# A fused attention and MLP block in fp32 on one core: the first T tile moves to second place in a unit's first step, and ScalarE copies the outputs of the last unit but one

## The chip, the cores and the metric

The kernel runs on one core of a Trainium2 chip. The engines that matter here are TensorE (PE in the profile, its weight loads PEld), VectorE (DVE), ScalarE (ACT), GpSimd (POOL) and SyncE (SP), which issues most DMAs. The metric is the device time of one execution in microseconds, the median of several runs. The kernel before took 1554.22 us (three runs, 1554.19 to 1554.6).

## The reference

```python
xn = layernorm(x)                                # 2048 tokens x 512
q, k, v = split(xn @ wqkv)                       # 32 heads of 16
o = softmax(q @ k.T * 16**-0.5) @ v              # per head, 2048 x 2048 scores
s = o @ wo
g = silu(gelu(xn @ w1 + b1) @ w2 + b2)           # 512 -> 1376 -> 512
return x + s * g
```

All of it is fp32. The scores are large, so the softmax subtracts each row's maximum, and the kernel therefore makes every score twice: once to take the maximum, once, transposed, for the exponential.

## The kernel before, in words

The program is written in a fixed order by hand; no scheduler moves anything. It has two stretches.

The first, up to about 470 us, does the layer norm, the projections and the MLP, and on the side a part of the first scores with their maxima. The second is a loop over n = 0 to 512, one step each. The heads are in 8 groups of four, the queries in 4 chunks of 512; a group and a chunk make a unit u (32 units), and a unit has 16 steps, one for each block of 128 keys. n = 16u is the first step of unit u.

A step is a string of letters (`ORDER`, and `FIRST` in the first step of a unit), each letter one piece of work for TensorE and what follows from it:

- **T** (four in a step, `t_one`, L713): 128 keys x 512 queries of transposed scores of one head, with the negated maximum as two more rows of the contraction. They go to the PSUM banks `ps` (the first T, here T0), `two` (T1 and T2 together) and `pst` (T3). ScalarE takes the exponential of each bank into a buffer `slot` (L716, L718). T0 and T2 use the lower 64 rows of TensorE's array (`SIDES`, second number 1), T1 and T3 the upper 64.
- **S** (L192): a whole 128 x 512 tile of scores of a later unit, whose row maxima VectorE takes (L198). In a step of three such tiles the first S (S0) is on the upper rows, the second (S1) on the lower.
- **X** and **Y** (L192): two half tiles of 256 columns, X on the upper rows, Y on the lower, in one bank; the reduction comes after Y. Ahead of Y a TensorE nop waits for X to be done (`hold`).
- **V** (`pv_step`, L784): probabilities times values of the step before, four matmuls side by side in the bank `pv`, summed over the 16 steps of a unit.

S, X and Y share three banks in a ring, so each of them waits until VectorE has reduced what stood in its bank. The sums in `pv` are complete with the V of step 16u, which belongs to unit u - 1; they are copied to `os` (L791), and the V of step 16u + 1 may only start when that copy is done, since there is one bank `pv`. The first T0 and the first T1 of a unit also wait for the DMAs that loaded its queries and maxima (`qt`), four DMA queues each; these waits are instructions of TensorE's own queue (EVENT_SEMAPHORE).

How many score tiles a step has is set by `due`: three in nearly every step up to n = 490, none after that. `FIRST` is used where a unit's first step has three, that is in units 5 to 30, 26 times. In the first steps of units 1 to 4 there are two, and the order is `ORDER[2]`, which begins with T.

From n = 492 on, without score tiles, the steps hold products with the output weights for the first ten token blocks instead (`w_halves`, L911), with ScalarE's rounding copies (L889) and tanh (L845), VectorE's gates (L846, L917) and GpSimd's differences and sums (L892, L922). The last copy of `pv` but one, that of unit 30, falls in step 496.

```python
ORDER = {0: "TTTTV", 2: "TSTTSTV", 3: "XTSTTYSTV"}
SIDES = ((1, 1), (0, 0), (0, 1), (1, 0))
        order = ORDER[want] if n > 1 else ("TTTTV", "TSTTSVT")[n]
        if want == 3 and ka == 0:
            order = FIRST
```

Of the kernel before, what the change touches and what calls it, by code (L numbers as in the profile page):

```python
# [10 lines left out]
AF = mybir.ActivationFunctionType  # L11
# [27 lines left out]
HB = 4  # L39
W2B = 2  # L40
ORDER = {0: "TTTTV", 2: "TSTTSTV", 3: "XTSTTYSTV"}
FIRST = "SXTTTSYTV"
SOON = 580
FEW = 4
SIDES = ((1, 1), (0, 0), (0, 1), (1, 0))
# [8 lines left out]
def fused(ctx: ExitStack, tc: tile.TileContext, x, wqk, wv, wo, w1, b1, w2, b2, out):  # L54
    nc = tc.nc
# [43 lines left out]
    NU = NG * NCH  # L99
# [677 lines left out]
    PV, OS, DN, DR = {}, {}, {}, {}  # L777
    def pv_step(u, k):
        g = u // NCH
        if k == 0:  # L780
            PV[u] = ps_v.tile([P, CH], F32, name="pv")
        for j in range(GH):
            h = (g * GH + j) * VW
            nc.tensor.matmul(PV[u][32 * j:32 * j + 32, :], vsb[:, k, h:h + 32], PT[u, k][:, j, :],  # L784
                             start=(k == 0), stop=(k == NT - 1))
        del PT[u, k]
        if k == NT - 1:
            OS[u] = wb.tile([P, CH], F32, name="os", bufs=1)
            pv = PV.pop(u)
            if u < NU - 1:  # L790
                nc.vector.tensor_copy(OS[u], pv)  # L791
            else:
                nc.scalar.activation(OS[u][:, :HC], pv[:, :HC], AF.Copy)
                nc.vector.tensor_copy(OS[u][:, HC:], pv[:, HC:])
# [189 lines left out]
    for n in range(L + 1):  # L984
        ua, ka = divmod(n, 16)
        want = due(n) - due(n - 1)
        i = 0
        if put_off and ka > 1:
            s_turn(*put_off.pop(0))
        else:  # L990
            for u in list(ended):
                if u >= PAIRED or ka > 2 and since.setdefault(u, n) < n:
                    s_end0(u)
# [3 lines that stand above are left out]
        for op in order:  # L997
            if op in "SXY":
                s_op(op)
            elif op == "V":  # L1000
                if n:
                    pv_step(*divmod(n - 1, 16))
                for _ in range(4):
                    tick()
                flush()
            else:
                if EARLY <= 4 * n + i < 4 * L:
                    t_one(ua, ka, i, True)
                for f, args in todo.get((n, i), []):
                    f(*args)  # L1010
                i += 1
# [54 lines left out]
```

## Time and profile before

| | |
|---|---|
| median of the runs | 1554.22 us |
| the profiled execution | 1554.05 us |
| its span, first to last instruction | 1552.3 us |
| granted TensorE clock, mean | 1.000 |
| busy: PE, DVE, ACT, POOL | 1544.9, 1415.1, 1214.2, 367.7 us |

The profiled execution lies within 0.2 us of the median, and 1.75 us of its time lie outside the span. Busy times of PE are no sign of a full TensorE, since matmuls overlap and their ends are modelled. A row of the timeline gives the start in us, the busy time of the row, engine, line, operation, output and input tile, shape and count; in square brackets stands the idle time of the engine ahead of the row and what ended it. Rows of the same kind that overlap are put together (x2). A row of the waits gives who waited for whom, us in total, times, longest.

### The profile page before, as it was taken

What the parts mean: (1) busy time and instruction counts of PE and PEld (TensorE: products, weight loads), DVE (VectorE), ACT (ScalarE), POOL (GpSimd) and SP (SyncE); (2) the same over time, 40 slices, a digit from 0 to 9 for tenths busy, and PEclk for the clock granted to TensorE, in tenths of its full rate; (3) what the DMA queues carried; (4) which work ended last, traced back from release to release, by engine and by line L of the source; (5) the groups of instructions that cost most, each with busy time, mean ns of one, the idle gap of its engine ahead of it and who ended that gap; (6) DMA issues with size and microseconds to landing.
All of it is one profiled execution on the core that took longest, in us unless ns stands there. A gap on an engine that the chain in (4) does not pass through costs nothing.

```text
span 1552.3 us, 31308 instructions
## 1 busy us (share of the span) xinstructions
PE 1544.9 (100%) x12242; PEld 926.8 (60%) x12242; DVE 1415.1 (91%) x2295; ACT 1214.2 (78%) x1881; POOL 367.7 (24%) x370
## 2 busy tenths in 40 slices
PE   9999999999999999999999999999999999999999
PEld 8899999999994444444444444444444444444455
DVE  7599999999998999999999999999999999999834
ACT  4333433434339999999999999999999999999984
POOL 4145675765741001001000100100010000000143
PEclk9999999999999999999999999999999999999999
DMA  6625443454422113113311411411041111110153
GB/s 211 154 60 146 129 140 100 145 152 122 130 85 77 44 36 67 30 37 61 66 28 30 70 37 36 69 34 29 23 81 29 33 30 32 41 30 22 48 197 115
DMA packets 78643, 116.83 MB, mean 75 GB/s; under 512 B 28036, under 2 KB 28292, under 8 KB 77320
## 3 DMA queue, kind: packets, MB, share of 16 engines
q1 hardware_dynamic: 74748, 101.89, 23.8%
q0 software_dynamic: 3264, 12.35, 4.7%
q8 instruction: 96, 1.57, 0.4%
q10 hardware_dynamic: 484, 0.60, 0.1%
q14 instruction: 51, 0.42, 0.1%
HBM read 84.35 MB, written 25.97 MB: 71 GB/s over the span
## 4 chain that ended last, share of the span: by engine, by line
PE 98%; DVE 1%; DMA 0%; ACT 0%; issue 0%; DVEq 0%
PE pv L784 33%; PE ps L192 22%; PE ps L582 13%; PE two L713 8%; PE sp L582 5%; PE pst L713 4%; PE ps L713 4%; PE pst L582 3%; PE pv L582 2%; PE ps L911 2%; PE ps L91 1%; PE ps L454 1%; PE pst L91 0%; DVE st L413 0%; PE two L91 0%; DMA xt<-in_x 0%
## 5 line engine op out<-in xcount | busy, mean ns | idle before, releaser
L198 DVE TENSOR_REDUCE mx<-ps 128x2 f32<-128x512 f32 x2048 | 1318.5, 687 | 75.3 <-PE ps L192 25.8
L784 PE MATMUL pv<-slot,vsb 128*32 128x512 f32 x4096 | 545.4, 605 | 0.9 <-DVE os L791 0.9
L718 ACT ACTIVATE slot<-two 128x1024 f32<-128x1024 f32 x511 | 520.4, 1018 | 4.3 <-PE pst L713 3.7
L192 PEld LDWEIGHTS ps<-kt,slot 48*128 48x128 f32 x1364 | 214.2, 185 | 295.8 <-DVE mx L198 285.0
L192 PE MATMUL ps<-kt,slot 48*128 48x256 f32 (+1 forms) x1364 | 374.8, 364 | 0.0
L716 ACT ACTIVATE slot<-ps 128x512 f32<-128x512 f32 x515 | 307.1, 597 | 18.0 <-PE ps L713 6.6
L716 ACT ACTIVATE slot<-pst 128x512 f32<-128x512 f32 x511 | 309.5, 606 | 0.6 <-PE ps L713 0.6
L582 PE MATMUL ps<-slot,w1h 64*128 64x512 f32 x1088 | 222.9, 393 | 0.0
L713 PE MATMUL two<-qt,kt 50*128 50x512 f32 x766 | 202.4, 399 | 0.3 <-DVE gt L642 0.3
L192 PE MATMUL ps<-kt,qz 48*128 48x512 f32 x512 | 202.5, 396 | 0.0
L713 PE MATMUL ps<-qt,kt 50*128 50x512 f32 x387 | 190.4, 494 | 0.0
L192 PEld LDWEIGHTS ps<-slot,slot 48*128 48x128 f32 x594 | 93.7, 184 | 126.3 <-DVE mx L198 121.5
L192 PE MATMUL ps<-slot,slot 48*128 48x256 f32 (+1 forms) x594 | 164.8, 364 | 0.0
L582 PEld LDWEIGHTS ps<-slot,w1h 64*128 64x128 f32 x1088 | 155.0, 186 | 8.8
L784 PEld LDWEIGHTS pv<-slot,vsb 128*32 128x32 f32 x4096 | 80.9, 108 | 131.0 <-issue 121.4
L582 PE MATMUL ps<-slot,w1l 64*128 64x512 f32 x544 | 155.1, 393 | 0.0
L713 PE MATMUL pst<-qt,kt 50*128 50x512 f32 x383 | 154.9, 405 | 0.0
L367 ACT ACTIVATE hg<-ps,b_sb 128x512 f32<-128x512 f32 x44 | 27.9, 684 | 134.7 <-PE ps L582 123.3
L374 POOL TENSOR_TENSOR hl<-hg,hh 128x512 fp32r<-128x512 f32 x76 | 96.8, 1296 | 153.2 <-ACT hh L373 107.4
L713 PEld LDWEIGHTS two<-qt,kt 50*128 50x128 f32 x766 | 114.8, 186 | 2.6 <-DVE gt L642 0.7
L245 POOL CAST mh<-nt 128x32 fp32r<-128x32 f32 x19 | 4.0, 209 | 394.0 <-DVE nt L243 329.3
L192 PEld LDWEIGHTS ps<-kt,qz 48*128 48x128 f32 x512 | 93.9, 183 | 0.9 <-DVE mx L198 0.6
(194 smaller groups left out, 1954.5 us busy)
## 6 DMA issues: line engine op xcount, KB each, us to landing
raw<-in_w SPq DMA_DIRECT2D x88, 256.0 KB
qk_h<-hh SPq DMA_DIRECT2D x32, 256.0 KB
qk_l<-hl SPq DMA_DIRECT2D x32, 256.0 KB
qt<-qk_h SPq DMA_DIRECT2D x128, 64.0 KB
slot<-qk_h SPq DMA_DIRECT2D x92, 64.0 KB
g_d<-gt POOLq DMA_DIRECT2D x16, 256.0 KB, 3.6
qt<-qk_l SPq DMA_DIRECT2D x64, 64.0 KB
dn<-den_d SPq DMA_DIRECT2D x32, 128.0 KB
```

What stands on the lines that cost most here:

```text
L91: nc.tensor.matmul(ps, lhs[a], rhs[b], start=first and n == 0, stop=last and n == 2)
L192: return nc.tensor.matmul(ps[:, c0:c0 + w], QS[u][r, p, qi * P:(qi + 1) * P], kts[u // NCH % KB][p][r, k0:k0 + w], start=True, stop=True).ins
L198: nc.vector.tensor_reduce(MX[u][:, 2 * p:2 * p + 2, qi, ki][:, heads, parts], ps.rearrange("p (n c) -> p n c", c=HC), axis=AX.X, op=OP.max)
L367: nc.scalar.activation(raw, ph.pop(u), AF.Gelu_apprx_tanh, bias=b1_sb[:, u[2]:u[2] + 1])
L374: nc.gpsimd.tensor_sub(hl, raw, hh.bitcast(F32))
L454: nc.tensor.matmul(pq["q", g, c], W1[g][i][:, k * P:(k + 1) * P], (xh, xl)[j][c][:, k], start=n == 0 and k == 0, stop=n == 2 and k == KT - 1)
L582: i = nc.tensor.matmul(ps, lhs[r], rhs[r], start=first, stop=last).ins
L713: nc.tensor.matmul(ps, kts[g % KB][p][r, k * P:(k + 1) * P], QT[u][r, p, :], start=True, stop=True)
L716: nc.scalar.activation(PT[u, k][:, 2 * p + a, :], ps, AF.Exp, scale=SCALE)
L718: nc.scalar.activation(PT[u, k][:, :2], TP["two"], AF.Exp, scale=SCALE)
L784: nc.tensor.matmul(PV[u][32 * j:32 * j + 32, :], vsb[:, k, h:h + 32], PT[u, k][:, j, :], start=(k == 0), stop=(k == NT - 1))
L911: HALF[0] = nc.tensor.matmul(PW[i][0], OTS[i, k][x][r], (wo_h, wo_l)[y][r, k], start=k == 0 and side == 0 and n == 0, stop=k == KT - 1 and ...
```

## The change

In a unit's first step, T0 and X change places: T0 is the second piece of the step instead of the third. For unit 30 alone, the copy of `pv` to `os` goes from VectorE to ScalarE.

```diff
-FIRST = "SXTTTSYTV"
+FIRST = "STXTTSYTV"
...
             pv = PV.pop(u)
-            if u < NU - 1:
+            if u < NU - 2:
                 nc.vector.tensor_copy(OS[u], pv)
+            elif u < NU - 1:
+                nc.scalar.activation(OS[u], pv, AF.Copy)
             else:
```

On TensorE, the first step of unit 6 (n = 96) shows the first part; the other 25 are alike. `pv` in the first row is the V of step 95, `kt_612` and `slot_4446` belong to the score tiles S0 (512) and X (256), `qt_617` with `kt_113` to T0 (`ps`) and T1 and T2 (`two`).

```order
 L784 MATMUL pv<-slot_9331,vsb 32x512 x4
 L192 MATMUL ps<-kt_612,slot_4446 128x512 [waits DVE_49]
-L192 MATMUL ps<-kt_612,slot_4446 128x256 [waits DVE_49]
 L713 MATMUL ps<-qt_617,kt_113 128x512 [waits DMAHW4_49,DMAHW3_49,DMAHW6_49,DMAHW2_49,Activation_49]
+L192 MATMUL ps<-kt_612,slot_4446 128x256 [waits DVE_49]
 L713 MATMUL two<-qt_617,kt_113 128x512 [waits DMAHW5_49,DMAHW1_49,DMAHW7_49,DMAHW0_49,Activation_49]
 L713 MATMUL two<-qt_617,kt_113 128x512
```

T0 with its five waits now stands ahead of X and of X's wait for VectorE; everything else keeps its place.

On ScalarE, step 496 shows the second part. The rows are the exponentials of steps 496 and 497 (`slot_20279`, `slot_20315`), with the rounding copy `oh` and a tanh (`slot_20163<-gx`) between; before:

```order
L716 ACTIVATE slot_20279<-pst 128x512 [waits PE_49]
L889 ACTIVATE oh<-slot_6842 128x512 [waits Pool_49]
L845 ACTIVATE slot_20163<-gx 128x512 [waits DMAHW0_49]
L716 ACTIVATE slot_20315<-ps 128x512 [waits PE_49]
L718 ACTIVATE slot_20315<-two 128x1024 [waits PE_49]
```

and with the change (the lines are two further down):

```order
L716 ACTIVATE slot_20279<-pst 128x512 [waits PE_49]
L891 ACTIVATE oh<-slot_6842 128x512 [waits Pool_49]
L847 ACTIVATE slot_20163<-gx 128x512 [waits DMAHW0_49]
L793 ACTIVATE os<-pv 128x512 [waits DMAHW3_49,DMAHW2_49,DMAHW4_49,DMAHW1_49,DMAHW5_49,DVE_49,PE_49]
L716 ACTIVATE slot_20315<-ps 128x512 [waits PE_49]
L718 ACTIVATE slot_20315<-two 128x1024 [waits PE_49]
```

The copy stands behind the tanh and ahead of the exponentials of step 497, which now come after it.

On VectorE, at the same place, the copy stood behind the gate (L846) that waits for that tanh:

```order
L917 SCALAR_TENSOR_TENSOR gx<-ps,gx 128x512 [waits DVE_49]
L846 SCALAR_TENSOR_TENSOR gx<-slot_20163,gx 128x512 [waits DMAHW0_49,Activation_49]
L791 COPY os<-pv 128x512 [waits DMAHW4_49,DMAHW3_49,DMAHW5_49,DMAHW2_49,PE_49]
L846 SCALAR_TENSOR_TENSOR gx<-slot_20163,gx 128x512 [waits DMAHW2_49,Activation_49]
L812 RECIPROCAL dr<-dr 128x16 [waits DMAHW0_49]
```

With the change the L791 row is gone, and the gates follow one another.

## The prediction

> **What bounds the kernel now.** I read the page's busy times first, then the waits, then the timeline of single steps, since every engine but POOL is nearly full and shares of a span decide nothing here. One row of the page, and one of ScalarE's waits between 620 and 1446 us:
>
> ```profile
> PE 1544.9 (100%) x12242; PEld 926.8 (60%) x12242; DVE 1415.1 (91%) x2295; ACT 1214.2 (78%) x1881; POOL 367.7 (24%) x370
> ```
>
> ```profile
> ACT slot L716 <- PE ps L713: 4.8, 27, 0.2
> ```
>
> The second row is all that ScalarE waits for there, 0.18 us at the first step of each unit: its exponential waits for T0, which `FIRST` puts behind S0 and X. But ScalarE is not what sets the step there. An ordinary step in TensorE's timeline (step 121):
>
> ```profile
> 712.35 0.39 PE L192 MATMUL ps<-kt,slot 48*128 48x256 f32 x1
> 712.35 0.50 PE L713 MATMUL ps<-qt,kt 50*128 50x512 f32 x1
> ...
> 713.04 0.39 PE L713 MATMUL pst<-qt,kt 50*128 50x512 f32 x1
> 713.04 0.39 PE L192 MATMUL ps<-kt,slot 48*128 48x512 f32 x1
> 713.37 1.06 PE L784 MATMUL pv<-slot,vsb 128*32 128x512 f32 x8
> 714.36 0.39 PE L192 MATMUL ps<-kt,slot 48*128 48x256 f32 x1
> ```
>
> X and T0 start together, on different rows of the array; the tiles take 1.02 us until `pv`, `pv` takes 1.0, the step 2.01. The first step of unit 7 (step 112) and the three after it:
>
> ```profile
> 693.89 0.50 PE L192 MATMUL ps<-kt,slot 48*128 48x512 f32 x1
> 694.09 0.46 PE L713 MATMUL ps<-qt,kt 50*128 50x512 f32 x1
> 694.24 0.27 PE L192 MATMUL ps<-kt,slot 48*128 48x256 f32 x1
> 694.35 0.47 PE L713 MATMUL two<-qt,kt 50*128 50x512 f32 x2
> 694.63 0.43 PE L713 MATMUL pst<-qt,kt 50*128 50x512 f32 x1
> 694.66 0.51 PE L192 MATMUL ps<-kt,slot 48*128 48x512 f32 x2
> 695.10 1.06 PE L784 MATMUL pv<-slot,vsb 128*32 128x512 f32 x8
> 696.10 0.38 PE L192 MATMUL ps<-kt,slot 48*128 48x256 f32 x1
> ...
> 698.12 0.39 PE L192 MATMUL ps<-kt,slot 48*128 48x256 f32 x1
> ...
> 700.26 0.38 PE L192 MATMUL ps<-kt,slot 48*128 48x256 f32 x1
> ```
>
> The first step lasts 2.21 us (693.89 to 696.10), the next 2.02, the third 2.14 (698.12 to 700.26): a unit's start loses 0.20 us in its first step and 0.13 in its third. These are the two stalls that the first part can act on. The second part acts on one stall, at 1485.6 us, below.
>
> **The first step, part by part.** Its burst of tiles takes 1.21 us instead of 1.02. T0 starts 0.20 late, although its rows of the array are free. The weight loads of this step, then TensorE's semaphore waits in this step and in the first step of unit 2, then VectorE up to the burst:
>
> ```profile
> 693.89 0.29 PEld L192 LDWEIGHTS ps<-kt,slot 48*128 48x128 f32 x2 [0.84 <-DVE mx L198]
> 694.06 0.18 PEld L713 LDWEIGHTS ps<-qt,kt 50*128 50x128 f32 x1
> ...
> 694.47 0.18 PEld L192 LDWEIGHTS ps<-kt,slot 48*128 48x128 f32 x1
> 694.57 0.18 PEld L713 LDWEIGHTS pst<-qt,kt 50*128 50x128 f32 x1
> ```
>
> ```profile
> L713 PEldq EVENT_SEMAPHORE  x4: 51/51/51, 693.9 to 694.2; - x4
> L713 PEldq EVENT_SEMAPHORE  x4: 51/51/51, 530.3 to 531.2; - x4
> ```
>
> ```profile
> 692.53 1.89 DVE L198 TENSOR_REDUCE mx<-ps 128x2 f32<-128x512 f32 x3
> ```
>
> The four DMA waits of T0 and T1 (first row of the second group) run from 693.9 to 694.2, during the burst. They stand behind X, and X waits for a reduction of VectorE. The row below is unit 2, whose first step (from 531.72 us) begins with T: there the same four run 1.4 to 0.5 us ahead of the burst, hidden behind `pv`. The change sends T0's two ahead of X, so T0 can load with S0, at 693.9; T1's two stay behind X. T0's start moves from 694.09 to 693.89, and ScalarE's wait of 0.18 us goes.
>
> The end of the burst gains less. S1 is next on T0's rows but one, and its load (694.47) comes 0.05 us after the reduction that frees its bank ends (last row: 692.53 + 1.89 = 694.42). That does not move. A load takes 0.11 us (the first row: two loads of 0.18 in 0.29), so S1 can start at 694.58 instead of 694.66, and `pv` 0.08 us earlier. T3's load (694.57) stays too, since it stands behind the wait for X; started at 694.68, with the 0.33 us that T3 takes to `pv` in the ordinary step, it allows `pv` at 695.01, 0.09 earlier. So the first step gains 0.08 us of its 0.20.
>
> What is late next is VectorE, which reduces three tiles, copies `os`, and reduces three more; below it a weight load of the third step, and VectorE in the first step of unit 2:
>
> ```profile
> 694.43 1.95 DVE L198 TENSOR_REDUCE mx<-ps 128x2 f32<-128x512 f32 x3
> 696.30 0.68 DVE L791 COPY os<-pv 128x512 f32<-128x512 f32 x1
> 696.90 1.88 DVE L198 TENSOR_REDUCE mx<-ps 128x2 f32<-128x512 f32 x3
> ```
>
> ```profile
> 698.83 0.18 PEld L192 LDWEIGHTS ps<-kt,slot 48*128 48x128 f32 x1
> ```
>
> ```profile
> 532.28 1.29 DVE L198 TENSOR_REDUCE mx<-ps 128x2 f32<-128x512 f32 x2
> ```
>
> The three after the copy are back to back, (1.88 - 0.68) / 2 = 0.60 us apart; the last ends at 698.78, and 0.05 later S1 of the third step loads. So the loss of the third step is the copy's backlog, and the unit gains only what VectorE gains. Its chain begins with the reduction of S0 at 694.43, 0.54 us after the burst's start. S0 does not move. Three reductions back to back put the copy at 694.43 + 1.80 = 696.23 instead of 696.30: 0.07 us. T0 beside S0 may delay S0: in step 32, where they start together at 531.72, the reduction comes at 532.28, 0.56 after, 0.02 more. That leaves 0.05 to 0.07. I take 0.06, between these two rows, and keep 0.04 to 0.09 (the upper end is the gain of the burst). 26 units: **1.6 us** (1.0 to 2.3). The rest of T0's head start is lost in waiting, and ScalarE's time saved is idle time. SP's and POOL's queues are not touched here.
>
> **The copy of unit 30.** In the stretch from 1470 us on a step takes 3.06 us, set by TensorE. One does not; TensorE, ScalarE and VectorE around it:
>
> ```profile
> 1483.54 0.49 PE L713 MATMUL ps<-qt,kt 50*128 50x512 f32 x1
> ...
> 1486.52 1.06 PE L784 MATMUL pv<-slot,vsb 128*32 128x512 f32 x8 [0.85 <-DVE os L791]
> 1487.52 0.50 PE L713 MATMUL ps<-qt,kt 50*128 50x512 f32 x1
> ...
> 1489.58 1.06 PE L784 MATMUL pv<-slot,vsb 128*32 128x512 f32 x8
> ```
>
> ```profile
> 1483.83 0.63 ACT L845 ACTIVATE slot<-gx 128x512 f32<-128x512 f32 x1
> 1484.35 0.60 ACT L716 ACTIVATE slot<-ps 128x512 f32<-128x512 f32 x1
> 1485.00 1.03 ACT L718 ACTIVATE slot<-two 128x1024 f32<-128x1024 f32 x1
> ```
>
> ```profile
> 1484.49 1.37 DVE L846 SCALAR_TENSOR_TENSOR gx<-slot,gx 128x512 f32<-128x512 f32 x1 [3.62 <-ACT slot L845]
> 1485.79 0.68 DVE L791 COPY os<-pv 128x512 f32<-128x512 f32 x1
> ```
>
> A later step reaches `pv` 2.06 us after its first T (1487.52 to 1489.58). From 1483.54 that is 1485.60; it came at 1486.52, 0.92 late, because the copy stood behind a gate that waited for ScalarE's tanh (1483.83) and then took 1.37 us. On ScalarE the copy starts after the tanh, at 1484.35, and takes the 0.60 us of the exponential of that shape: done at 1484.95, 0.65 us before `pv` needs it. Behind it the exponentials of step 497 move by 0.50 (0.60 less the 0.10 by which neighbours overlap): `ps` to 1484.85, `two` to 1485.35, ended at 1486.38. The next step's T1 needs bank `two` at 1485.60 + 1.0 = 1486.60, so 0.2 us of cover is left, and ScalarE waits for TensorE again in that step. If that cover is short, TensorE waits for what is missing, at most the copy's 0.50. So **0.92 us** (0.4 to 0.95). The five DMAs of `os` on SP leave about 1.5 us earlier and wait for nothing new; nobody needs them sooner.
>
> **The sum** is 1.6 + 0.9 = 2.5 us. The profiled execution (1552.3 us span, 1554.05 in all) would come to 1551.5; the median of the runs, 1554.22, to **1551.7**. Own range 1551.0 to 1552.7. 0.2% of this kernel, 3.1 us, is about what a measurement can tell from no change; the bound lies at 1551.1.
>
> **Rivals.**
>
> - ScalarE becomes the bound at step 497, so that the copy costs there what it saves on VectorE. For it speaks that ScalarE is much the fuller of the two:
>
> ```profile
> 1487.52:1530.00 42.48, 42.48 (x340) 22.38 (x338) 16.60 (x22) 38.61 (x61) 19.26 (x14) 1.00 0.54 181
> ```
>
>  The columns are PE, PEld, DVE, ACT, POOL: 16.6 us on VectorE, 38.6 on ScalarE, of 42.5. Against it: one copy meets one step, and the cover above. With 0.5 us paid back, the time is 1554.2 - 1.6 - 0.4 = 1552.2. The Trainium skill (Perfetto Trace Analysis, Optimizing Scalar/DVE Operations) has the rule that work either engine can do may go to Scalar where DVE is saturated; in this stretch DVE is not, so by that rule the copy moves the wrong way and this rival is the result. I weigh the row of the one wait higher than the row of the shares.
> - VectorE's chain is not the limit of the third step after all, and the first step falls to an ordinary one: 26 x (2.21 - 2.01) = 5.2 us, and 0.9: 1548.1. For it, T0's full 0.20 us; against it the 0.05 us between reduction and load, twice.
> - The first part does nothing: S0's delay by T0 eats all of 0.07 us. 1554.2 - 0.9 = 1553.3.
> - Slower: T0 and S0, started together, do not run beside each other but one after the other, and S0 is reduced a tile later. A tile of 512 costs some 0.23 us (T1 or T2 to T3, 694.35 to 694.63, less 0.05); VectorE's chain then loses 0.23 - 0.07 = 0.16 us a unit, 26 x 0.16 = 4.2, less 0.9: 1557.5. It decides from a delay of S0's reduction of 0.07 us on for a loss in the part, and of 0.22 for a slower kernel. Step 32 speaks against it, with 0.02.
>
> **Chances.** The sum as worked out 0.57, about a third of that beyond 1551.1, since VectorE's gain is known to 0.02 us and counts 26 times; ScalarE bound 0.10; full gain 0.12; first part nothing 0.11; slower 0.10. Faster: 0.12 + 0.18 = 0.30. Within: 0.39 + 0.10 + 0.11 = 0.60. Slower: 0.10. The range 1549.4 to 1554.0 leaves out the slower case and a part of the full gain.
>
> **What would show it.** Right: ScalarE's waits for `ps` nearly gone; T0 within 0.01 us of S0; bursts of 1.13 us in the first steps; third steps still 2.13 to 2.16 long; no wait of `pv` at 1485.6. Wrong: S0's reduction more than 0.57 us after the burst's start; first steps of 2.02; a wait of T1 for bank `two` at about 1486.6.

## The result and the profile after

The changed kernel takes 1551.81 us (median of 20 runs, 1551.04 to 1552.98), the kernel before beside it 1554.52 (20 runs, 1553.9 to 1555.74): a ratio of 0.9982, with a 95% interval of 0.9976 to 0.9988, or 2.7 us. The forecast was 1551.7. The profiled execution took 1551.71 us, with a span of 1549.9 against 1552.3 before.

The page's busy times and ScalarE's waits between 620 and 1446 us, after the change:

```profile
PE 1543.7 (100%) x12242; PEld 922.4 (60%) x12242; DVE 1413.0 (91%) x2294; ACT 1214.4 (78%) x1882; POOL 367.7 (24%) x370
```

```profile
ACT slot L716 <- PE ps L713: 3.8, 23, 0.2
```

In the first row the counts show one copy less on DVE and one activation more on ACT. The busy sums moved by other amounts (DVE by 2.1 us, where a copy takes 0.68), and the shares not at all: they don't tell where 2.7 us went. The second row was to be nearly empty; the half copy below tells why it is not.

**The first step of unit 7 and the two after it**, TensorE's timeline after the change, to be set beside the rows from 693.89 on in the prediction:

```profile
693.79 0.49 PE L192 MATMUL ps<-kt,slot 48*128 48x512 f32 x1
693.79 0.50 PE L713 MATMUL ps<-qt,kt 50*128 50x512 f32 x1
694.12 0.28 PE L192 MATMUL ps<-kt,slot 48*128 48x256 f32 x1
...
694.36 0.50 PE L192 MATMUL ps<-kt,slot 48*128 48x512 f32 x1
694.48 0.48 PE L713 MATMUL pst<-qt,kt 50*128 50x512 f32 x1
694.70 0.27 PE L192 MATMUL ps<-kt,slot 48*128 48x256 f32 x1
694.90 1.06 PE L784 MATMUL pv<-slot,vsb 128*32 128x512 f32 x8
695.90 0.38 PE L192 MATMUL ps<-kt,slot 48*128 48x256 f32 x1
...
697.91 0.39 PE L192 MATMUL ps<-kt,slot 48*128 48x256 f32 x1
...
700.08 0.38 PE L192 MATMUL ps<-kt,slot 48*128 48x256 f32 x1
```

T0 (second row) starts with S0, where it had been 0.20 us late. `pv` comes 1.11 us after the burst's start instead of 1.21, the step takes 2.11 us instead of 2.21, the next 2.01, the third 2.17 instead of 2.14. TensorE's semaphore waits for T0 and T1 in this step, the weight load of S1, and VectorE from the reduction of S0 on:

```profile
L713 PEldq EVENT_SEMAPHORE  x4: 51/51/51, 693.2 to 693.9; - x4
```

```profile
694.36 0.18 PEld L192 LDWEIGHTS ps<-kt,slot 48*128 48x128 f32 x1
```

```profile
694.32 1.89 DVE L198 TENSOR_REDUCE mx<-ps 128x2 f32<-128x512 f32 x3
696.12 0.68 DVE L791 COPY os<-pv 128x512 f32<-128x512 f32 x1
```

T0's two waits now run 0.63 and 0.52 us ahead of the burst, hidden behind the last `pv`; T1's two, which still stand behind X, run from 0.03 us ahead of it to 0.13 us into it. The reduction of S0 starts 0.53 us after the burst's start (694.32 - 693.79), before 0.54; the copy 2.33 us after it (696.12 - 693.79), before 2.41 (696.30 - 693.89). The copy now follows back to back (694.32 + 1.80 = 696.12), where it had come 0.07 us late. The means over the 26 units are the same within 0.01: first step 2.213 us before and 2.118 after, second 2.018 and 2.016, third 2.139 and 2.160, copy at 2.415 and 2.338. Per unit 0.076 us are gained. From the start of step 80 to the start of step 495 the changed kernel takes 2.07 us less than the kernel before.

**Step 497**, the place of the second part, on TensorE and on ScalarE:

```profile
1481.55 0.50 PE L713 MATMUL ps<-qt,kt 50*128 50x512 f32 x1
...
1483.62 1.07 PE L784 MATMUL pv<-slot,vsb 128*32 128x512 f32 x8
1484.62 0.49 PE L713 MATMUL ps<-qt,kt 50*128 50x512 f32 x1
...
1486.68 1.06 PE L784 MATMUL pv<-slot,vsb 128*32 128x512 f32 x8
1487.68 0.50 PE L713 MATMUL ps<-qt,kt 50*128 50x512 f32 x1
```

```profile
1481.88 0.63 ACT L847 ACTIVATE slot<-gx 128x512 f32<-128x512 f32 x1
1482.40 0.60 ACT L793 ACTIVATE os<-pv 128x512 f32<-128x512 f32 x1
1482.87 0.61 ACT L716 ACTIVATE slot<-ps 128x512 f32<-128x512 f32 x1
1483.35 1.04 ACT L718 ACTIVATE slot<-two 128x1024 f32<-128x1024 f32 x1
```

The copy ends at 1483.00, 0.62 us ahead of `pv`, which follows the first T by 2.07 us as in the next step (1484.62 to 1486.68); the 0.85 us wait is gone, and the step takes 3.07 us instead of 3.98 (1483.54 to 1487.52). No tile waits for bank `two`: the step after it is 3.06 us long, as all are there. From the start of step 495 to the end of step 497 the program gains 0.92 us.

**The tail** gave some of it back in this one execution. The last rows of the chain that ended last, before and then after:

```profile
1529.26 1.96 PE pv L784 x16
...
1537.00 9.99 PE ps L91 x48
1546.99 1.44 PE two L91 x12
```

```profile
1526.37 1.99 PE pv L784 x16
1529.26 2.85 DMA dr<-os
1532.42 1.60 DMA den_d<-dr
1534.04 4.29 DMA dn<-den_d
...
1544.65 1.44 PE two L91 x12
```

The last `pv` starts 2.89 us earlier (2.07 + 0.92, less the 0.09 us by which step 80 began later in this execution), but from there to the end of the span it is 23.53 us instead of 23.04: the three small transfers of the last unit's sums stand in the chain, where before TensorE's matmuls hid them (the stretch from ScalarE's last copy of `pv` to VectorE's product that needs them was 9.58 us before and is 10.12). In the seven experiments below, with the same tail, the stretch from the last `pv` on is 22.96 to 23.3 us, and TensorE is its chain each time; six of them hold the copy of unit 30 on ScalarE, and five a changed order with it. This points at the one execution, and not at the change.

### The profile page after: what moved, and what is told of

It is laid out like the page before. It is cut to its first block, busy times and chain, and to the rows that moved or that the text cites. A ratio compares the mean times of both kernels' runs of the same rounds, so it can differ in the third digit from the quotient of the medians.

```text
span 1549.9 us, 31307 instructions
## 1 busy us (share of the span) xinstructions
PE 1543.7 (100%) x12242; PEld 922.4 (60%) x12242; DVE 1413.0 (91%) x2294; ACT 1214.4 (78%) x1882; POOL 367.7 (24%) x370
## 4 chain that ended last, share of the span: by engine, by line
PE 98%; DVE 1%; DMA 1%; ACT 0%; issue 0%; DVEq 0%
PE pv L784 33%; PE ps L192 22%; PE ps L582 13%; PE two L713 8%; PE sp L582 5%; PE ps L713 4%; PE pst L713 4%; PE pst L582 3%; PE pv L582 2%; PE ps L913 2%; PE ps L454 1%; PE ps L91 1%; DVE st L413 0%; DMA dn<-den_d 0%; DMA xt<-in_x 0%; DMA dr<-os 0%
```

## The experiments

**Each part alone.** First the order without the copy:

```diff
-FIRST = "SXTTTSYTV"
+FIRST = "STXTTSYTV"
```

> Only FIRST is changed; all copies of pv but the last unit's stay on VectorE. By the working of the prediction, with the sizes of the trace after (26 units, about 0.075 us each): 1.9 us faster than before, and step 497 still 3.98 us long. Rival, the copy carries all of the gain: no difference to before.

Measured: 1552.01 us (10 runs) against 1554.02 of the kernel before (25 runs), ratio 0.9987 [0.9977, 0.9996]. First steps take 2.121 us, third ones 2.156, the copy comes 2.339 us after the burst's start; steps 80 to 495 gain 1.96 us. At step 497 nothing is gained (4.01 us), and `pv` waits there as before:

```profile
1483.99 1.07 PE L784 MATMUL pv<-slot,vsb 128*32 128x512 f32 x8 [0.87 <-DVE os L791]
```

Then the copy without the order:

```diff
-            if u < NU - 1:
+            if u < NU - 2:
                 nc.vector.tensor_copy(OS[u], pv)
+            elif u < NU - 1:
+                nc.scalar.activation(OS[u], pv, AF.Copy)
```

> Only the copy of unit 30 goes to ScalarE; FIRST is as before. Theory: 0.9 us faster than before, step 497 3.06 us, first steps of units 2.21 and third steps 2.14 us as before. Rival, ScalarE pays the copy back: 0.4 us or less.

Measured: 1553.34 us (10 runs), ratio 0.9994 [0.9985, 1.0004]; 0.7 us by the medians, which alone would not tell it from nothing, but 0.92 us in steps 495 to 497 of the trace, where the place is seen by itself, with a step 497 of 3.06 us. First and third steps are as before (2.212, 2.141). The two parts do not touch each other, and their sum, 1.96 + 0.92, is the 2.07 + 0.92 of the changed kernel to 0.1. How far such a comparison of two traces can be trusted is seen here too: steps 80 to 495, in which this kernel is the kernel before, take 0.24 us longer, and the two kernels with the new order differ there by 0.11.

**Is it VectorE's chain that sets the unit, or TensorE's first step?** The order of an ordinary step starts with X, and T0's DMA waits then stand behind a tile that need not wait for the last reduction:

```diff
-FIRST = "STXTTSYTV"
+FIRST = "XTSTTYSTV"
```

> The changed kernel with FIRST = XTSTTYSTV, the order of every other step. X then waits for an earlier reduction, so T0 should start within 0.01 us of the burst's start although it stands behind X, and the first step should shrink to 2.02 us. But the first reduction of the unit then comes 0.66 us after the burst's start instead of 0.53. Theory, VectorE's chain sets the unit: its copy comes 0.12 us later, the third step takes 2.38 us, and the kernel is 3 us slower than the changed one, about as fast as before. Rival, TensorE's first step sets it: 26 x 0.10 us = 2.6 us faster than the changed kernel.

Measured: 1554.02 us (10 runs), ratio 1.0001 [0.9992, 1.0011]. TensorE's timeline in the first step of unit 7 and the two after it, and VectorE's from the first reduction of that step on:

```profile
693.52 0.38 PE L192 MATMUL ps<-kt,slot 48*128 48x256 f32 x1
693.52 0.50 PE L713 MATMUL ps<-qt,kt 50*128 50x512 f32 x1
...
694.54 1.07 PE L784 MATMUL pv<-slot,vsb 128*32 128x512 f32 x8
695.54 0.39 PE L192 MATMUL ps<-kt,slot 48*128 48x256 f32 x1
...
696.71 1.06 PE L784 MATMUL pv<-slot,vsb 128*32 128x512 f32 x8
697.71 0.38 PE L192 MATMUL ps<-kt,slot 48*128 48x256 f32 x1
...
699.93 0.39 PE L192 MATMUL ps<-kt,slot 48*128 48x256 f32 x1
```

```profile
694.17 1.89 DVE L198 TENSOR_REDUCE mx<-ps 128x2 f32<-128x512 f32 x3
695.98 0.68 DVE L791 COPY os<-pv 128x512 f32<-128x512 f32 x1
```

and the weight loads of the V of the second step:

```profile
696.71 0.16 PEld L784 LDWEIGHTS pv<-slot,vsb 128*32 128x32 f32 x8 [0.41 <-DVE os L791]
```

T0 starts with X, and the first step is an ordinary one, 2.02 us: TensorE has regained all that the first step lost. But the first tile that VectorE can reduce is the second one made (S0), 0.65 us after the burst's start instead of 0.53. The copy comes 2.46 us after it instead of 2.33, the V of the second step waits for it (its step takes 2.17 us), and the third takes 2.22. Steps 80 to 495 lose 1.03 us against before and 3.1 against the change, which is 26 times the 0.12 us by which the copy comes later. I had looked for the loss in the third step alone (2.38); it splits over two. The rival "full gain of the first step" falls with this: a first step of 2.02 us is worth nothing if it puts the reductions later.

**Is the third step's loss the copy's backlog?** VectorE copies 256 of the 512 columns; the other half of the copy is left out for units 0 to 29, and GpSimd fills those columns with ones.

```diff
-                nc.vector.tensor_copy(OS[u], pv)
+                nc.vector.tensor_copy(OS[u][:, :HC], pv[:, :HC])
+                nc.gpsimd.memset(OS[u][:, HC:], 1.0)
```

> The changed kernel, with VectorE copying only the first 256 of the 512 columns of pv for units 0 to 29; the other 256 are left out (GpSimd fills them with ones). The copy then takes 0.43 us instead of 0.68. Theory, the third step's loss is the backlog of the copy: the third step falls from 2.16 to 2.02 to 2.04 us, 26 x 0.13 = 3.4 us faster than the changed kernel. Rival, the third step is long for another reason: no difference.

Measured: 1547.48 us (4 runs), ratio 0.9958 [0.9943, 0.9972]. VectorE in the first step of unit 7, and ScalarE's waits between 620 and 1446 us:

```profile
693.73 1.89 DVE L198 TENSOR_REDUCE mx<-ps 128x2 f32<-128x512 f32 x3
695.54 0.41 DVE L791 COPY os<-pv 128x256 f32<-128x256 f32 x1
695.97 1.89 DVE L198 TENSOR_REDUCE mx<-ps 128x2 f32<-128x512 f32 x3
```

```profile
ACT slot L716 <- PE ps L713: 0.2, 1, 0.2
```

The reductions follow the copy after 0.43 us instead of 0.60, and the third step falls from 2.160 to 2.014 us, an ordinary step; the first stays at 2.116. Steps 80 to 495 gain 3.7 us more than with the change, 26 x 0.142. ScalarE's waits have gone too, so in the changed kernel they belong to the third step's loss: 21 of its 23 stand in the step after the third, while 26 of the 27 before stood in the first. ScalarE at the step after the third, in the kernel before and in the changed one:

```profile
700.05 0.61 ACT L716 ACTIVATE slot<-pst 128x512 f32<-128x512 f32 x1
700.80 0.60 ACT L716 ACTIVATE slot<-ps 128x512 f32<-128x512 f32 x1
```

```profile
700.62 0.60 ACT L716 ACTIVATE slot<-ps 128x512 f32<-128x512 f32 x1 [0.16 <-PE ps L713]
```

Before, the engine was idle here for 0.14 us (700.05 + 0.61 to 700.80), and the view names no wait; now it is 0.16, and it does. Means over units 6 to 27: the idle time ahead of this exponential was 0.136 us and is 0.157, that of the first step was 0.177 and is 0.045.

**Would ScalarE hide the other copies as it hides that of unit 30?** All copies but the last unit's go to ScalarE:

```diff
-            if u < NU - 2:
-                nc.vector.tensor_copy(OS[u], pv)
-            elif u < NU - 1:
+            if u < NU - 1:
                 nc.scalar.activation(OS[u], pv, AF.Copy)
```

> The changed kernel with the copies of pv of all units but the last on ScalarE. VectorE's chain loses 0.60 us a unit, so by that alone the third step would be 2.02 us, 26 x 0.15 = 3.8 us faster than the changed kernel. Theory: ScalarE, with 0.1 us of slack a step, hands on the copy's 0.5 us as late exponentials; T3 of the third step waits for bank pst and the step takes about 2.3 us, 4 us slower than the changed kernel. Rival, the copy is as well hidden on ScalarE as in unit 30: 3.8 us faster.

Measured: 1555.51 us (10 runs) against 1553.63 of the kernel before on that chip (19 runs), ratio 1.0012 [1.0003, 1.0021]: slower than the changed kernel by 4.7 us as the ratios have it, and by 3.6 between steps 80 and 495. ScalarE around the copy of unit 6 in step 112, whose burst began at 694.44, and TensorE's load of T3 two steps on:

```profile
696.88 0.62 ACT L791 ACTIVATE os<-pv 128x512 f32<-128x512 f32 x1
697.36 0.63 ACT L716 ACTIVATE slot<-ps 128x512 f32<-128x512 f32 x1
...
698.74 0.66 ACT L716 ACTIVATE slot<-pst 128x512 f32<-128x512 f32 x1
```

```profile
699.45 0.18 PEld L713 LDWEIGHTS pst<-qt,kt 50*128 50x128 f32 x1
```

ScalarE now runs back to back, the exponentials of the second step come at 2.92 us after the burst's start instead of 2.64 (696.43 - 693.79 in the changed kernel), and the last of them ends at 699.40, 0.05 us before T3 of the third step loads for the same bank `pst`: third steps take 2.296 us. VectorE is relieved of 30 more copies than with the change, and that buys nothing, since the third step now hangs on ScalarE. At step 497 the same move is free: the step there is 3.06 us long, and the exponential of `two` behind the copy ends 0.23 us before the next step begins (1484.39 and 1484.62 in the changed kernel).

**Does it matter that S0 stays first?** T0 ahead of S0, as in unit 2, whose reduction had served as the bound:

```diff
-FIRST = "STXTTSYTV"
+FIRST = "TSXTTSYTV"
```

> The changed kernel with FIRST = TSXTTSYTV: T0 ahead of S0. In step 32 of the kernel before, where T0 is first, the first reduction came 0.56 us after the burst's start, in the changed kernel 0.53. If the place of S0 behind T0 makes that difference, VectorE's chain is 0.03 us later a unit and the kernel about 0.8 us slower than the changed one. If it is the unit 2's own tiles that make it, no difference.

Measured: 1551.79 us (10 runs), ratio 0.9991 [0.9981, 1.0] on the same chip as the last. VectorE from S0's reduction on, with the burst at 693.03:

```profile
693.60 1.89 DVE L198 TENSOR_REDUCE mx<-ps 128x2 f32<-128x512 f32 x3
695.40 0.68 DVE L791 COPY os<-pv 128x512 f32<-128x512 f32 x1
```

The reduction comes 0.57 us after the burst's start (mean 0.570, in the changed kernel 0.534), the copy 0.036 us later, the third step takes 2.191 us. Steps 80 to 495 gain 1.32 us instead of 2.07: 0.029 us a unit for one place in the queue. The medians can't show so little. The step starts can, though 0.75 us is only three times the 0.24 by which two like traces differed; the firmer sign is the delay itself, in the means over 26 units.

**Half a copy on each engine**, the version to which the two last experiments on the copy point:

```diff
             if u < NU - 2:
-                nc.vector.tensor_copy(OS[u], pv)
+                nc.vector.tensor_copy(OS[u][:, :256], pv[:, :256])
+                nc.scalar.activation(OS[u][:, 256:], pv[:, 256:], AF.Copy)
```

> The copies of units 0 to 29 are cut in two halves of 256 columns: VectorE takes the first, ScalarE, ahead of the next step's exponentials, the second. If the two engines could read the bank pv side by side, ScalarE's half would start at 2.44 us after the burst's start and take the 0.39 us of the half copy of unit 31, its exponentials would be some 0.25 us late (in the kernel with all copies on ScalarE 0.48), and the third step would fall to about 2.05 us: 26 x 0.11 = 2.9 us faster than the changed kernel, about 1549. In unit 31, where the copy is cut in this way already, VectorE's half starts 0.03 us after ScalarE's has ended (1528.38 + 0.39, then 1528.80). My theory: here too one waits for the other, ScalarE for VectorE, which begins at 2.34; ScalarE's half starts at 2.8, its exponentials of the second step at about 3.1 instead of 2.64, later than with all copies on ScalarE (2.92), and the third step is 2.3 to 2.5 us long: 4 to 9 us slower than the changed kernel, 1555.5 to 1560.5.

Measured: 1558.76 us (8 runs) against 1553.65 (11 runs), ratio 1.0032 [1.0021, 1.0042]. ScalarE and VectorE in the first step of unit 7, where the burst began at 695.56:

```profile
698.35 0.38 ACT L792 ACTIVATE os<-pv 128x256 f32<-128x256 f32 x1 [0.22 <-DVE os L791]
698.63 0.59 ACT L716 ACTIVATE slot<-ps 128x512 f32<-128x512 f32 x1
```

```profile
697.89 0.42 DVE L791 COPY os<-pv 128x256 f32<-128x256 f32 x1
```

ScalarE waits until VectorE's half is done (697.89 + 0.42, then 698.35), so the exponentials of the second step come at 3.07 us, later than with the whole copy on ScalarE (2.92). Second steps take 2.10 us and third ones 2.32. The 0.142 us a unit that the half copy showed to be there are not to be had in this way. The row in brackets is a wait for a semaphore; whether the two engines could read the bank side by side without that wait was not tried.

## Why the prediction was right

- **T0's DMA waits go ahead of X and hide behind `pv`.** So it came: T0's two start 0.63 and 0.52 us ahead of the burst, T0 3 ns after S0. T1's two stayed behind X, as the prediction had it.
- **The first step gains 0.08 us.** 0.095 came, and for the reason given. S1's load stays where it was, 0.58 us after the burst's start in the mean over the 26 units, before and after, and the 0.11 us for the load is there, but inside the row. S1's row now starts with its load (694.36, both rows). It lasts 0.49 us, where before, with the weights loaded 0.20 us ahead, it lasted 0.39; and Y follows S1's start by 0.34 us instead of 0.23. So S1 gets to its work at about 0.69 (0.58 + 0.11), as worked out, and not where its row begins. `pv` follows Y by 0.21 us in both kernels. The term was 0.015 us too small.
- **VectorE's chain sets the unit, at 0.06 us each.** The mechanism was right: X first, T0 ahead of S0 and a half copy all move the unit the way VectorE's chain says. The term was a little too small: 0.076 us came. The 0.02 that I took off for T0 beside S0 came from step 32, and there S0 stands behind T0 in the queue. With T0 behind S0 the reduction is not later at all (0.534 us against 0.536), and with S0 behind T0 it is 0.036 later. So the copy gained the whole 0.077 us, and 26 units gave 2.0 us instead of 1.6, within the 1.0 to 2.3. Third steps were to stay at 2.13 to 2.16 us; they take 2.160.
- **The copy of unit 30 saves 0.92 us.** 0.92 came. The cover for bank `two` sufficed: the exponential of `two` ends at 1484.39 (1483.35 + 1.04), 0.23 us before the next step begins, where 0.2 had been worked out.
- **The sum** was 2.5 us and is 3.0 in the loop, 2.7 by the medians. With 1551.81 the time lies 0.1 us from the forecast, and on the side of no measurable difference by the bound of 3.1 us, which had 0.6. That it lies so near is partly luck: the loop gained 0.5 us more than was worked out, and the kernel before, run beside it, took 1554.52, 0.3 us more than the 1554.22 from which the sum was taken.
- **ScalarE's waits nearly gone: wrong as a sign.** They fell only from 4.8 us in 27 to 3.8 in 23. The step that failed is the reading of that row as all that ScalarE waits for. The idle time of the first step did go, from 0.177 us to 0.045. But one of 0.136 us, in the step after the third, was there already and stood in no row; with the third step 0.02 us longer it is 0.157, and the row counts it. No idle time below 0.15 us appears in any row here. For the time it did not matter, since ScalarE does not set these steps.
- **The rivals.** ScalarE as the bound at step 497: no, the 0.92 us came whole and the next step is an ordinary one. The full gain: refuted by the order with X first. The first part nothing: refuted by the order alone. S0 and T0 one after the other: S0's reduction did not move.

## What to carry to other kernels

In a loop in which several engines are full, a stall that is removed is worth what the engine that is late next gains by it, and not its own length: here 0.20 us on TensorE became 0.076, through VectorE's chain, and an order that gave TensorE the whole 0.20 threw the gain away again, 3 us against the changed kernel. Which engine should take a movable piece of work was told here not by their shares but by what stands behind it at that place: one copy on ScalarE saved 0.92 us, thirty more cost about 4 us. And where an effect is a fraction of a microsecond, compare the starts of the same steps in two traces, with two traces of like code beside them to see how far they differ by themselves; the medians of whole runs can't show it.

## What the runs showed of the hardware

The waits for DMAs in TensorE's queue take 51 ns each, and two that follow each other start 0.11 us apart (0.63 and 0.52 us ahead of the burst of step 112). They hold what is behind them, but they ran ahead where nothing ahead of them was blocked: the same two waits cost 0.20 us behind a tile that waits for VectorE, and nothing half a microsecond earlier.

A matmul's row that starts together with its weight load lasts 0.10 us longer than one whose weights were loaded 0.20 us ahead (S1: 0.49 and 0.39 us), so the start of a row alone does not tell when a tile is done.

Of two tiles that start within 4 ns of each other on different rows of the array, the first in the queue is not slowed by the second (S0's reduction at 0.534 us after the burst's start with T0 behind it, 0.536 without), and the second is reduced 0.036 us later. And in the kernel before, the profile has T0 start ahead of X (694.09 and 694.24) in all 26 units although X stands ahead of it in the program: on different rows, a matmul that stands behind another in the program can start first.
